# A gated linear attention with a token mixer: the third of four batches also loaded and computed in token pairs

## The chip, the cores and the metric

The kernel runs on one core of a Trainium2 chip. The metric is the device time of the whole kernel in microseconds (us); before the change the median of three runs is 162.89 us (162.86 to 162.95). The profile that is read here is of one execution and spans 162.7 us from its first to its last instruction.

The core's engines work side by side, each in its own order: TensorE (PE) for matrix products, VectorE (DVE), ScalarE (ACT) and GpSimd (POOL) for the rest, and SyncE (SP), which issues most of the transfers between the chip's memory and the on-chip buffer. Matrix products go to eight banks of the accumulation memory (`ps`), from which the other engines take them.

## What is computed

Two stages, one behind the other, for 4 batches, 8 heads, 768 tokens and 48 values a head (384 in all), everything in 32-bit floats at the outside:

```python
# stage 1: a decaying state per head
for t in range(S):
    state = alpha[:, :, t, :, None] * state + einsum('bhd,bhe->bhde', k[:, :, t], v[:, :, t])
    y[:, :, t] = einsum('bhd,bhde->bhe', q[:, :, t], state)
# stage 2: x is y as [batch, token, head*48]
h = x.transpose(0, 2, 1) @ U @ V          # low rank (32) mixing over tokens
u = x + h.transpose(0, 2, 1)
out = u + maximum(u @ w_ch1, 0) @ w_ch2   # 384 -> 1536 -> 384
```

q, k, v and alpha lie in memory as [batch, head, token, 48]. One token of one head is a run of 48 x 4 = 192 bytes; two neighbouring tokens of one head are a run of 384 bytes.

## The kernel before

Stage 1 is done in chunks of 128 tokens. With the logarithms of alpha summed over the chunk, exp(-sum) scales k and exp(sum) scales q; a masked score product of the two gives what tokens of one chunk give each other, and a state of the chunks before is added. There are two forms of this, chosen batch by batch:

```python
PAIR = (0, 1)      # batches in pair units
HALF = (0, 1)      # of these, the ones with products split over the two halves of the array
ROWS = (1, 2, 3)   # how the mixing of a batch is laid out
TRD = {(3, c): "kq" for c in range(NC)}   # last batch: kT and qT by transposing DMAs, not on TensorE
```

The loads of both forms, 192 KB each:

```python
def load(t, src, c):
    if b in PAIR:      # half the heads, two chunks; a partition holds two neighbouring tokens
        hs, sl = slice((c % 2) * HP, (c % 2 + 1) * HP), slice((c // 2) * 2 * C, (c // 2 + 1) * 2 * C)
        ... dma_start(t().rearrange("p (h j) d -> p h (j d)", j=2),
                      src[b, hs, sl, :].rearrange("h (p j) d -> p h (j d)", j=2))       # L411
        return
    sl = slice(c * C, (c + 1) * C)      # all heads, one chunk; a partition holds one token
    ... dma_start(t(), src[b, :, sl, :].rearrange("h t d -> t h d"))                    # L418
```

A unit of the chunk form (`stage_gla`) on TensorE, six to a batch: the sums (L685, one product of 384 columns, and L687, the totals, four of one column), the transposes of the scaled k and q (L743, four each; in the last batch a DMA instead, L734), the scores (L759, eight in two tiles at a time), the state products (L782, four), the old state's part (L849, four) and the chunk's own part of the output (L851, eight). VectorE masks the scores (L769) and ScalarE, VectorE and GpSimd share the rest.

A unit of the pair form (`stage_pair`), also six to a batch (three blocks of two chunks by two halves of the heads). Even and odd tokens are two halves of a tile, and so a sum over tokens needs products among them:

```python
def f_cum(e):
    l2 = jh(lt()[:, :, 0:D])
    nc.tensor.matmul(... lhsT=upto, rhs=l2[:, 0:1].to_broadcast([C, 2, HP, D]), start=True, stop=False)  # L461, 384 columns
    nc.tensor.matmul(cb()[:, 0:Q], lhsT=below, rhs=l2[:, 1], ...)                                         # L462, 192
    nc.tensor.matmul(cb()[:, Q : 2 * Q], lhsT=upto, rhs=l2[:, 1], ...)                                    # L463, 192
    ...                                                                                                   # L470, totals, four
```

Then the transposes (L507), the scores (L531, sixteen small products, four tiles at a time), the state products (L570, eight in two row tiles), the unit's own part of the output (L617, sixteen in two row tiles) and the old states' part (L629, two for each of the two chunks). Two states of half the heads are kept in place of one of all; sums and scalings of states, and the copies of the output, are twice as many and half as wide (L604, L590, L340 and L338).

Stage 2 of a batch: the mixing (L869, L903, L911, L926), then `mlp1` (L953, three products of 384 columns for each of 24 results, evicted to h1t by L963 or L965), then `mlp2` (L983, twelve products a chunk), the addition of u (L995), and the store. A batch in pair form is stored in two halves, even and odd tokens apart:

```python
if b not in PAIR:
    P.add(..., lambda e, lo=lo, hi=hi: nc.sync.dma_start(out[b, c * C : (c + 1) * C, lo:hi], ou()[:, lo:hi]), ...)   # L1002
    continue
for z in range(2):
    def f_store(e, z=z): ...                                                                                       # L1009
```

All operations are first listed and then issued in the order of a table of numbers, `TABLE`. A letter behind a number picks ScalarE (A), VectorE (V) or GpSimd (G) where there is a choice. The order is searched with a model of costs outside the kernel; each engine carries out its part of the table strictly in that order. Loads go into 36 buffers (`io`, 192 KB each), shared with the weights. Until 28 us of the plan, TensorE is given products without use (L331) in its gaps.

Of the kernel before, what the change touches and what calls it, by code (L numbers as in the profile page):

```python
# [156 lines left out]


TABLE = """
75 2 3 4 5 209 211 67 76 163 165 79 234 214 167 69 77 68 170V 212 215G 236 217 172 238 213 216V 166 169V 218 171 174V 220V 173V 175 176 83 70 81 237  # L160
168 219A 71 78 164G 80 178 221 179 223 73 72 87 74 0 241G 180 222 181 84 186 259 239 188 210G 240G 190 189 261 224 225 226 177 264 263 192V 1 193G 187G
242 227 243 244A 262 245V 229 230 231 194 246 232V 282 191 196A 233V 228 247 248 182 195 284 197A 184A 201 198 183 85 287 285 265G 82 88 202 266V 267
203 269A 235G 89 268 199 204 200 86 270A 185A 286 249 250 251 271 90 91 7 288G 254 289V 8 260G 95 6 33 99 252 256 35 31 23 39 10 290 258A 253 272 273
292A 19 41 21 37 27 25 107 29 291 255 205 274 275 293A 276 294 257A 295 296 283A 277 57 297 298 279 206 9G 410 34G 32G 412 278 299 208A 207V 300 301
302 304V 101 92 100 47 96 97 94 415 280A 281A 303A 13 16 305 306 93 43 55 45 49 14A 311 308 314 317 307A 51 63 59 53 456 315 309 433 98 103 312 17V
313A 458 318 320 310V 323 321 324 322V 325V 435 11 20V 319V 36A 316A 340 338 342 362 339V 61 436 461 438 341A 366 22G 42G 364 24A 460 363A 12A 38V 40V
365V 352 328 437 367A 414 30A 459 65 102 111 108 104 109 105 329V 343V 26V 28V 463V 106 462G 326 348 349A 506 413 330 368 354 360 355V 331V 336 508
353V 416V 439V 112 346 332 511 347A 369A 333A 372 373V 334 335V 337V 327V 440G 358 356 465 344 464 467V 510 361A 509 359A 442 411G 417G 115 113 444V
345A 357A 466A 418 441 350 419 425 443V 420V 421V 351A 46A 48A 468 15 44G 56G 50G 110 114 426 469 445 422 370 116 424 423 446 470 371A 52A 380 386 54G
64G 429 430 432V 447 58A 431A 434A 374 375 448 452 62G 427 428V 449 60V 66V 450 387 381 453 454A 117 481 483 376 457V 455V 476 471 477 382 486 485 529  # L170
484 531 377 472 512G 514 388 473V 487V 513V 474 516V 515 392 489 488V 451G 383 532 533 517A 491V 479V 389 482G 490 478 492A 480A 535G 534 653 393 496
497 493 518 498G 536G 495 494 119 394 655 537 398 538 379 378 123 390 127 399 499 520 395 519 475G 500G 530G 507A 539A 656 659V 501 521 544 540A 658
657 541 660G 503 661 545 400 502 662A 505A 522 504A 663 542 543 524 547 523G 546V 664V 526 672 549 551A 548 525 550A 674 118 391 124 121 120 129 131
528V 135 133 122 125 527V 665 552 404 676 677 553A 675 692 712 554 654G 401 666 137 139 667 132 126 564 559 555 560 556 561 405 406 557 670 562 668 565
566 694 714 567 563V 669 558A 587 585 589 696 716 695 715 717 590A 732 671V 679V 568V 573 609 605 407 610V 698G 579 615 606V 616V 571 580A 586A 588A
752 591 734 592A 697 700 577 678V 572V 701V 754 673G 719G 699G 756 737 755 680 607 134 613 608V 578V 595 575 682 687 574V 681V 688 614V 611 576A 736
612A 596A 603 702 581 601 703V 689G 597 569 599 604A 582A 735 598A 570A 863 600A 602A 683V 128 385 136 384 408 758G 739G 693G 738G 704 684 705 685 686
583 707 617 740 722 584A 708 723V 718G 865 618 690 867 130 141 403 706 159 151 147 138 757G 709V 691V 866 741A 713G 619 710 761 762A 720 742 593 759
760A 594A 721V 629 620 143 409 146 396 621 622 402 868 727 743V 630 728 140 148 145 155 724 744 898 952 916 753A 733G 18 870G 729G 763 711V 765 726 764
635 636 745 725 746 631 623 747 637 900 901 624 730 750 748 749V 766 767V 632 880 731A 882 902 751A 883 903 885 884 872 625 869G 638 626 768 628 871  # L180
641 642 152 153 627 149 397 142 769V 780 775 776 770 777 771 781 782 643 918 919 772 887G 904G 647 954 648 778 783 649 773 889 920 779V 784V 144 634
150 811 922G 923G 934 956 955 812A 921 924 774V 829 813 873 787 830V 814V 160 874 799 800V 875 650 819 793 815 794V 644 816V 936 809 827 825 810V 823
791 828V 785 905G 881G 864G 886G 899G 788A 925 907 876 906 888 957G 824V 826V 786V 877 797 803 893 821 878 157 792A 798A 938 894 804V 156 154 161 805
806V 801 158 941V 802V 937 879A 939 822A 820A 817 926 890 908 940G 818A 928 959 789 790A 892 891 909 917G 895G 958G 853 910 795 796V 943 942 807 808V
896 831 911 912 833 854 935G 960 914 947 929 927 913V 930 931V 948 949V 915A 832A 858 834 835 859 633 162 855 953V 836 837 944 946 961 945 860 838 839
950 932 652 963 962 646 964 651 645 856 843 840 861 951V 933A 965A 897A 966 848 967A 841 978 968 973 980 975 974 979 844 849 970 969 845 976 977A 857
842 862 981 850 971 982V 1015 1016V 1025 1007 1011 1013 1027 972V 991 1008V 993 994A 1028A 1026A 851 846 1009 995 1001 999 1023 1002A 1014A 1024A 992A
1021 1019 1029 1022V 1012V 1017 1010A 1020A 1018A 983 1046 1047 1030V 1048 1049 984A 989 990V 987 1051 1005 1003 1004V 639 1050 985 1052 997 1053 986V
988V 1054 640 1055 852 996A 1031 1041 1036 998V 1042 1006A 1000A 1043 1044 1032 1037 1038 1033 1056 1045 847 1039 1040 1034 1057 1059 1060 1035 1058
1061  # L190
"""


# [5 lines left out]
def kernel(  # L199
# [12 lines left out]
    nc = tc.nc  # L212
    B, H, S, D = q.shape
    C = 128
    NC = S // C
    HP = H // 2
    DM = H * D
# [11 lines left out]
    def slots(name, n, shape, dtype):  # L229
        return [const.tile(shape, dtype, name=f"{name}{i}") for i in range(n)]  # L230

    PAIR = (0, 1)
    HALF = (0, 1)
    ROWS = (1, 2, 3)
    TOTD = ()
    INTR = ()
# [4 lines left out]
    P = Plan()  # L241
# [16 lines left out]
    for x in (filler, tri, ident, mask2, blocks):  # L258
        nc.vector.memset(x, 0.0)
    nc.gpsimd.affine_select(  # L260
        out=tri, in_=tri, compare_op=ALU.is_gt, fill=1.0, base=0, pattern=[[1, 2], [-1, C]], channel_multiplier=1
# [30 lines left out]
    for i in range(2):  # L292
        r = slice(64 * i, 64 * i + 64)
# [675 lines left out]
    def mlp2(b, xb, ub, utx, h1, c):  # L969
        tt = c // NT  # L970
        low = b in XT
        base = xb if low else ub
        ou = Buf(outs)
        parts = [(0, 256), (256, DM)] if b == B - 1 and c == NC - 1 else [(0, DM)]
        for n, (lo, hi) in enumerate(parts):
            hb = Buf(bank)
            groups = [range(NJ)] if len(parts) > 1 else [range(4 * g, 4 * g + 4) for g in range(3)]
            for g, jts in enumerate(groups):
                last = jts[-1] == NJ - 1

                def f(e, jts=jts, hb=hb, lo=lo, hi=hi, last=last):
                    for jt in jts:
                        nc.tensor.matmul(  # L983
                            hb()[:, 0 : hi - lo], lhsT=h1()[:, jt, c * C : (c + 1) * C], rhs=w2_sb[:, jt, lo:hi],
                            start=(jt == 0), stop=(jt == NJ - 1 and not low),
                        )
                    if low and last:
                        nc.tensor.matmul(hb()[:, 0 : hi - lo], lhsT=vp_sb[:, c * C : (c + 1) * C], rhs=utx()[:, lo:hi], start=False, stop=True)

                need = [(h1, tt, jt) for jt in jts] + [("w2", jt) for jt in jts] + ([utx] if low and last else [])  # L990
                cost = mm(*[hi - lo] * (len(jts) + (1 if low and last else 0)))
                P.add({"PE": cost}, f, r=need, w=[hb])

            def f_o(e, hb=hb, lo=lo, hi=hi):
                nc.vector.tensor_tensor(ou()[:, lo:hi], base()[:, c, lo:hi], hb()[:, 0 : hi - lo], op=ALU.add)  # L995

            P.add({"DVE": 70 + 398 * (hi - lo) // DM}, f_o, r=[hb] + (xk(b, xb, c) if low else [(ub, c)]), w=[(ou, n)])

            if b not in PAIR:
                P.add(  # L1000
                    {"SP": 550.0 * (hi - lo) / DM + (0 if len(parts) == 1 else 60)},
                    lambda e, lo=lo, hi=hi: nc.sync.dma_start(out[b, c * C : (c + 1) * C, lo:hi], ou()[:, lo:hi]),  # L1002
                    r=[(ou, n)],
                )
                continue
            for z in range(2):

                def f_store(e, z=z):
                    nc.sync.dma_start(out[b, c * C : (c + 1) * C, :].rearrange("(m j) x -> j m x", j=2)[z], ou()[64 * z : 64 * z + 64, :])  # L1009

                P.add({"SP": 300.0}, f_store, r=[(ou, n)])

    small()
    weights1()
# [49 lines left out]
```

## Time and profile before

| engine | busy us | share of the span |
|---|---|---|
| TensorE, products | 153.9 | 95% |
| TensorE, weight loads (beside the products) | 99.6 | 61% |
| VectorE | 119.3 | 73% |
| ScalarE | 85.4 | 52% |
| GpSimd | 52.8 | 32% |

The largest groups of TensorE are the two mlp lines: L983 (53.5 us for 300 products) and L953 (51.0 us for 288). Transfers moved 30.39 MB in 89,910 packets, of which 83,584 were under 512 bytes. A load of 192 KB lands 4.1 us after its issue (median), in either form.

How to read what follows. A busy time is the union of an engine's records; records of TensorE overlap, so that the mean record is longer than the distance from one product to the next. A wait is written as: engine, line, the one that released it, then the sum in us, how often, and the longest. In the order of time a line begins with the start and the length in us, then engine, line and operation, the buffers (out<-in), the shape and the count; idle time ahead of it stands in brackets. Names of buffers are written without their numbers: `io` is any input tile, `rk` and `rq` the scaled k and q, `kt` and `qt` their transposes, `pm` the masked scores, `st` a state, `h1t` the result of `mlp1`.

### The profile page before, as it was taken

The page shows a single profiled execution, that of the slowest core. Times are in us where ns is not written, and L with a number is a line of the kernel's source. Part 1 is how long each engine was busy: PE and PEld are TensorE (multiplying, and loading weights), DVE is VectorE, ACT ScalarE, POOL GpSimd, SP SyncE. Part 2 cuts the span into 40 slices and gives each one's busy share as a digit, 9 for nine tenths or more (in the row PEclk, how much of TensorE's full clock was granted, in tenths as well). Part 3 has the DMA queues.
Part 4 walks back from the last instruction along what each step waited for, and adds up shares of the span by engine and source line. Part 5 has one row for each costly group of instructions (what it writes and reads, how often), then busy time and mean ns, then how long its engine had stood idle before and what let it go on. Part 6 is the DMA issues. An engine that isn't in the chain of part 4 may idle for free.

```text
span 162.7 us, 4734 instructions
## 1 busy us (share of the span) xinstructions
PE 153.9 (95%) x1821; PEld 99.6 (61%) x1821; DVE 119.3 (73%) x275; ACT 85.4 (52%) x224; POOL 52.8 (32%) x85
## 2 busy tenths in 40 slices
PE   6899999999999999999999999896899999999992
PEld 2457677566666665766676657463576747666662
DVE  6289995788997999977487969696698777234441
ACT  5748788958836678676954661601701311472000
POOL 5256741217336460215975005533370000000000
PEclk9999999999999999999999999999999999999999
DMA  5999999998999967979988879999994631002223
GB/s 128 288 299 272 270 234 290 286 310 254 297 320 258 241 144 162 194 155 213 201 194 162 201 141 210 192 156 180 223 246 15 186 106 28 0 0 76 97 109 133
DMA packets 89910, 30.39 MB, mean 187 GB/s; under 512 B 83584, under 2 KB 89856, under 8 KB 89888
## 3 DMA queue, kind: packets, MB, share of 16 engines
q1 hardware_dynamic: 83360, 28.52, 73.9%
q10 hardware_dynamic: 6528, 1.57, 6.7%
q8 instruction: 14, 0.23, 0.6%
q14 instruction: 8, 0.07, 0.1%
HBM read 23.79 MB, written 4.72 MB: 175 GB/s over the span
## 4 chain that ended last, share of the span: by engine, by line
PE 67%; SPq 15%; DMA 12%; issue 2%; ACT 1%; DVE 1%; POOL 0%; ACTq 0%; DVEq 0%; POOLq 0%
PE ps L983 27%; PE ps L953 23%; SPq L411 10%; DMA io<-in_moe_w_ch_dram 4%; DMA io<-in_v_dram 4%; DMA qt<-rq 3%; DMA io<-in_q_dram 2%; PE ps L759 2%; PE ps L507 2%; PE ps L743 2%; SPq L387 2%; SPq L1009 2%; PE ps L926 1%; PE ps L851 1%; PE ps L531 1%
## 5 line engine op out<-in xcount | busy, mean ns | idle before, releaser
L983 PE MATMUL ps<-w_sb,h1t 128*128 128x384 bf16 (+2 forms) x300 | 53.5, 320 | 0.0
L953 PE MATMUL ps<-uT,w_sb 128*128 128x384 bf16 x288 | 51.0, 326 | 1.3 <-ACT h1t L963 0.9
L953 PEld LDWEIGHTS <-w_sb 128*128 128x128 bf16 x288 | 27.1, 98 | 17.8 <-issue 1.5
L983 PEld LDWEIGHTS <-h1t 128*128 128x128 bf16 x300 | 26.7, 98 | 16.0 <-issue 1.8
L963 ACT ACTIVATE h1t<-ps 128x384 bf16<-128x384 f32 x52 | 23.6, 497 | 20.7 <-PE ps L953 12.7
L965 DVE TENSOR_SCALAR h1t<-ps 128x384 bf16<-128x384 f32 x44 | 22.7, 552 | 11.1 <-PE ps L953 11.0
L769 DVE TENSOR_TENSOR pm<-ps,maskc 128x512 bf16<-128x512 f32 x24 | 15.1, 683 | 3.3 <-PE ps L759 3.3
L995 DVE TENSOR_TENSOR ou<-ub,ps 128x384 f32<-128x384 bf16 (+2 forms) x19 | 9.9, 528 | 9.2 <-PE ps L983 7.8
L542 DVE TENSOR_TENSOR pm<-ps,maskp 128x512 bf16<-128x512 f32 x24 | 15.6, 683 | 0.5 <-PE ps L531 0.5
L722 POOL TENSOR_TENSOR rk<-io,ai 128x384 bf16<-128x384 f32 x10 | 9.2, 923 | 19.1 <-DMA io<-in_k_dram 13.9
L342 POOL CAST rv<-io 128x384 bf16<-128x384 f32 x18 | 9.4, 527 | 16.5 <-DMA io<-in_v_dram 16.1
L338 ACT CAST xb<-ps 128x192 bf16<-128x192 f32 (+1 forms) x22 | 7.7, 377 | 12.7 <-PE ps L851 6.1
L492 POOL TENSOR_TENSOR rk<-io,ai 128x384 bf16<-128x384 f32 x7 | 6.8, 965 | 11.6 <-DMA io<-in_k_dram 7.3
L722 POOL TENSOR_TENSOR rq<-io,aa 128x384 bf16<-128x384 f32 x10 | 9.1, 914 | 4.2 <-DMA io<-in_q_dram 3.1
L911 DVE TENSOR_TENSOR ub<-xb,ps 128x384 bf16<-128x384 bf16 x18 | 8.6, 549 | 1.8 <-PE ps L903 1.8
L695 ACT ACTIVATE ai<-ps 128x384 bf16<-128x384 f32 x12 | 5.8, 498 | 4.9 <-PE ps L685 3.5
L441 ACT ACTIVATE lt<-io 128x384 bf16<-128x384 f32 x12 | 6.1, 524 | 3.6 <-DMA io<-in_alpha_dram 3.6
L342 POOL CAST w_sb<-io 128x384 bf16<-128x384 f32 x10 | 4.9, 509 | 9.4 <-DMA io<-in_moe_w_ch_dram 9.4
L696 ACT ACTIVATE aa<-ps 128x384 bf16<-128x384 f32 x12 | 5.8, 496 | 3.6 <-POOL rk L722 2.1
L338 ACT COPY kt<-ps 128x512 bf16<-128x512 bf16 x10 | 5.9, 587 | 3.0 <-PE ps L743 1.3
L492 DVE TENSOR_TENSOR rq<-io,aa 128x384 bf16<-128x384 f32 x7 | 4.5, 649 | 3.9 <-ACT aa L478 3.3
L676 ACT ACTIVATE lt<-io 128x384 bf16<-128x384 f32 x12 | 6.1, 522 | 2.0 <-DMA io<-in_alpha_dram 2.0
(133 smaller groups left out, 242.8 us busy)
## 6 DMA issues: line engine op xcount, KB each, us to landing
io<-in_alpha_dram SPq DMA_DIRECT2D x24, 192.0 KB, 4.1
io<-in_k_dram SPq DMA_DIRECT2D x24, 192.0 KB, 4.1
io<-in_q_dram SPq DMA_DIRECT2D x24, 192.0 KB, 4.2
io<-in_v_dram SPq DMA_DIRECT2D x24, 192.0 KB, 4.1
io<-in_moe_w_ch_dram SPq DMA_DIRECT2D x24, 192.0 KB, 4.1
out_dram<-ou SPq DMA_DIRECT2D x24, 96.0 KB, 3.2
out_dram<-ou SPq DMA_DIRECT2D x11, 192.0 KB, 1.9
out_dram<-ou SPq DMA_DIRECT2D x1, 128.0 KB, 1.7
```

What stands on the lines that cost most here:

```text
L338: nc.scalar.copy(dst, src)
L342: nc.gpsimd.tensor_copy(dst, src)
L411: lambda e: nc.sync.dma_start(t().rearrange("p (h j) d -> p h (j d)", j=2), src[b, hs, sl, :].rearrange("h (p j) d -> p h (j d)", j=2)),
L492: eng.tensor_tensor(jh(dst()[:, :, 0:D]), raw(a), jh(x()), op=ALU.mult)
L542: nc.vector.tensor_tensor(dst, s2, maskp.to_broadcast([C, 2, 2, C]), op=ALU.mult)
L722: eng.tensor_tensor(dst()[:, :, 0:D], a(), x(), op=ALU.mult)
L769: nc.vector.tensor_tensor(pm()[:, :, par, :], s2, maskc.to_broadcast([C, HP, C]), op=ALU.mult)
L953: nc.tensor.matmul(hb()[:, 0:TW], lhsT=w1_sb[:, ct, jt * 128 : (jt + 1) * 128], rhs=uT()[:, ct, tt * TW : (tt + 1) * TW], start=(ct == 0), ...
L963: nc.scalar.activation(dst, hb()[:, 0:TW], AF.Relu)
L965: nc.vector.tensor_scalar_max(dst, hb()[:, 0:TW], 0.0)
L983: nc.tensor.matmul(hb()[:, 0 : hi - lo], lhsT=h1()[:, jt, c * C : (c + 1) * C], rhs=w2_sb[:, jt, lo:hi], start=(jt == 0), stop=(jt == NJ - ...
L995: nc.vector.tensor_tensor(ou()[:, lo:hi], base()[:, c, lo:hi], hb()[:, 0 : hi - lo], op=ALU.add)
```

## The change

Batch 2 is loaded and computed in pair form too, and only batch 3 stays in whole chunks. It is meant to give the third batch's loads longer runs (384 in place of 192 bytes, 512 runs a load in place of 1024). As the number of operations goes from 1062 to 1095, the whole order was searched anew.

```diff
 TABLE = """
-75 2 3 4 5 209 211 67 76 163 165 79 234 214 167 69 77 68 170V 212 215G ...
+67 75 79 71 68 69 70 209 163 165 211 3 4 186 167 170V 76 83 80 168 166 ...
 [all lines of the table are replaced; cut]
 """
@@
-    PAIR = (0, 1)
-    HALF = (0, 1)
+    PAIR = (0, 1, 2)
+    HALF = (0, 1, 2)
     ROWS = (1, 2, 3)
@@
             for z in range(2):

-                def f_store(e, z=z):
-                    nc.sync.dma_start(out[b, c * C : (c + 1) * C, :].rearrange("(m j) x -> j m x", j=2)[z], ou()[64 * z : 64 * z + 64, :])
-
-                P.add({"SP": 300.0}, f_store, r=[(ou, n)])
+                def f_store(e, z=z, lo=lo, hi=hi):
+                    nc.sync.dma_start(out[b, c * C : (c + 1) * C, lo:hi].rearrange("(m j) x -> j m x", j=2)[z], ou()[64 * z : 64 * z + 64, lo:hi])
+
+                P.add({"SP": 20 + 280.0 * (hi - lo) / DM}, f_store, r=[(ou, n)])
```

The edit of the store changes nothing here: a result is written in two parts of its columns only in the last chunk of batch 3, which isn't in pair form, so lo:hi is the whole row for every batch in pairs.

What the tables ask for, read through the list of operations: batches 0 and 1 come first in both, with the same 25 loads ahead of the small inputs and the first weights; in both, TensorE goes to the first `mlp1` product of batch 0 after the whole first stage of batch 0 and the sums of three units of batch 1. Before, the score product of the first unit of batch 3 stands 18 groups of TensorE after the first group of the mixing of batch 2, after the change 8.

More of the change, by code (lines that the diff above doesn't have):

```diff
@@ L159 @@
 TABLE = """
[L160 to L187, printed above, removed]
@@ L188 @@
-1021 1019 1029 1022V 1012V 1017 1010A 1020A 1018A 983 1046 1047 1030V 1048 1049 984A 989 990V 987 1051 1005 1003 1004V 639 1050 985 1052 997 1053 986V
-988V 1054 640 1055 852 996A 1031 1041 1036 998V 1042 1006A 1000A 1043 1044 1032 1037 1038 1033 1056 1045 847 1039 1040 1034 1057 1059 1060 1035 1058
-1061
+67 75 79 71 68 69 70 209 163 165 211 3 4 186 167 170V 76 83 80 168 166 169V 164V 234 188 236 212 178 215V 213 214 171 237 238 259 173V 217 172 219V 179
+240V 77 174A 191 242 216G 261 244A 190 189 175 180 177 81 176 73 78 241G 218 193V 181 243 72 87 74 84 85 220A 264 262 82 210G 221 245A 195 246 263 239
@@ new lines @@
+5 224 225 88 192G 223 222 248 226 247 194 197A 282 284 227 228 89 86 187G 2 265G 90 91 229 201 196A 231 198 8 202 6 7 285 286 233A 230 232A 203 267
+266V 199 204 200 268 95 99 31 35 269A 235G 33 182 270A 287 249 250 184A 271 183 251 185A 288G 37 19 21 23 290 252 29 39 41 27 25 292A 289V 260G 283G
+291 273 272 293A 253 254 256 255 274 275 276 294 258A 257A 277 205 297 206 279 298 278 296 295 410 299 10 412 207V 208A 280A 413 281A 9G 300 301 302
+303V 13 16 305 32G 304A 101 93 100 53 92 36G 96 49 306 14V 17V 51 97 107 47 45 43 34G 308 323 320 317 57 55 63 65 94 98 59 61 307A 433 321 309 456 310V
@@ new lines @@
+22G 20G 24G 318 314 324 325A 311 312 315 322A 102 108 103 111 109 458 435 437 319V 366 316V 313V 459 460 367A 30A 461 438 342 40G 362 338 339A 436 340
+350 354 363V 341V 42A 1 38V 330 328 326 344 104 331V 345V 343V 415 28A 26G 355A 351A 332 358 370 333A 105 414 417G 0 463G 356 368 372 371A 373A 352
+359A 353A 336 337A 106 369V 416V 439V 360 419 418 465 329V 361V 462G 327A 357A 50A 421A 112 334 364 467V 440V 464 52G 441 466V 443V 442 348 48G 46G 44G
+56G 411G 60G 113 506 420A 335A 444V 349A 115 508 365V 468 114 422 445 470 469 346 510 509 54A 58A 386 380 64A 347A 511 66A 434A 446 447 424 423 110 387
@@ new lines @@
+374 375 425 429 116 431A 381 426 427 62V 452 448 117 449 457V 428V 450 451G 512G 430 382 481 454A 453 432A 455A 376 388 529 383 389 483 484 486 485 471
+472 377 476 477 514 531 119 390 391 127 118 379 513G 515 392 516A 473G 487V 517V 488V 489 534 532 479A 533 393 474 482V 490 11 121 122 132 135 142 491A
+123 378 120 478 535G 492V 496 12A 497 480V 518 493 394 536G 498G 520 494 495 499 519 537 653 475G 530G 539A 398 538 540A 655 399 656 658 657 541 395
+507G 500G 659V 501 521 544 660G 503 542 522 523G 543 661 502 400 504A 663A 505A 662 545 524 547 525 546V 548 526 549 654G 664V 676 527V 528V 678 550A
@@ new lines @@
+551A 665 552 404 668 667 666 401 136 126 131 124 137 139 129 128 402 403 125 679 680 553A 681 669 559 724 772 554 555 556 560 405 406 561 564 672 147
+557 674A 565 562 683V 563V 566 774 726 558A 575 685 776 727 728 729 777 699 775 567 130 159 407 687V 384 134 133 143 148 408 140 673 568V 576V 670 682V
+155 579 577 589 591 701 675V 141 592V 603 615 671G 778G 702 705G 18 580A 599 569 703 749 780 782A 700A 590V 613 614A 600V 779G 578V 585 146 138 144
+604V 151 677A 896 704 385 570V 684 581 595 781 571 686A 783A 616V 582V 593 597 573 609 707 572V 574V 598V 709V 15 706G 730G 583 596A 594A 931 586A 610A
@@ new lines @@
+708 584A 710V 714 691 715 692 716G 688 693 690 694G 731G 717 725G 718G 711 611 587 751 617 588A 754 753 612A 752 605 618 712 689 713 619 606A 396 397
+152 756V 695 719 739 696 758 620 740 697V 698A 760A 755G 741G 897G 742 743G 721 757 601 732 898 720 602V 733 735V 629 759A 734A 722A 901 784 723V 736
+761 750V 900 913 899 773G 902G 967 630 786 738 763 737 762 631 933 607 934 936 608A 904 949 935 635 744 764 787 785 632 636 637 745 746 937G 903G 747A
+788 765 766V 789V 638 767 790 951 769 792 768 915 791 771A 748A 623 153 409 145 793A 954 794V 770V 909 795 796V 918 905 916 639 150 157 622 910 624 149
@@ new lines @@
+625 626 627 160 158 640 621 161 802 797 647 648 649 917 985 952 953 914A 803 804 920V 799 798 919G 906 807 805 969 907 808 809 921 806A 970 800 641 642
+972 939 810 801V 938V 955V 811V 822 830 820 643 831V 908 644 856 926 821V 846 814 847V 823V 857V 650 815V 940 971 922 957 824 911 832 833V 848 912V 927
+840 850 987 816 838 854 841V 932G 956G 958 928G 944 945 989 988 825A 849A 634 156 628 646 990G 154 633 162 645 973G 991G 836 834 842 837V 851V 855A
+839A 817A 835A 941 942 974G 968G 959 923 843A 924 826 827V 925 858 812 818 819V 943 813V 852 950G 946G 844 884 845V 960 961 992 828 947 993 975 859A
@@ new lines @@
+976 962 860 885 980 890 963 964G 853V 981 965 861 891 829A 966A 948A 994 982G 986G 977 892 929 996 995 979 978 872 886 997 998V 893 983 866 862 930A
+984A 863 887 999 1000V 873 874 1011 1001 1006 1012 1008 888 889 652 651 867 878 879 1013 1014 1007 1009 868 1003 1002 1015A 1010V 880 869 881 1004 1056
+1050 1046 1005V 1024 1062 1057A 1025A 1063A 1051V 1047V 1018 1020 1054 1026 1040 1041V 1048 1049V 1021V 865 1036 1042 1032 1019A 1027V 1055V 1044 1022
+1052 1043V 1033V 1045A 1053A 1058 1034 1016 1017V 1030 894 864 1023A 1060 1061A 1031A 1074 1035V 1037V 1038 1028 1029V 875 1069 1079 1084 1080 1059V
@@ L191 @@
+1081 876 895 871 882 883 1039V 1082 877 1083 1064 1065 1066 1067 1068 1075 1070 1071 1076 1072 1077 870 1085 1086 1089 1092 1087 1078 1090 1088 1073
+1093 1091 1094
 """
```

## The prediction

> **What bounds the kernel now.** I read the page from the top: first the busy shares and the slices of part 2, then the chain that ended last, then the busy time by stretches, and last the waits and the order of time of single instructions.
>
> ```profile
> PE 153.9 (95%) x1821; PEld 99.6 (61%) x1821; DVE 119.3 (73%) x275; ACT 85.4 (52%) x224; POOL 52.8 (32%) x85
> ...
> PE   6899999999999999999999999896899999999992
> ...
> DMA  5999999998999967979988879999994631002223
> ...
> PE 67%; SPq 15%; DMA 12%; issue 2%; ACT 1%; DVE 1%; POOL 0%; ACTq 0%; DVEq 0%; POOLq 0%
> ```
>
> In the first row the reader sees TensorE near full; in the slices, that it dips in only two places, at the start and in the slices 26 to 28 (about 106 to 118 us), and that both lie where the DMA row is near full. The chain says the same: two thirds of it TensorE, the rest transfers and their issue. The stretches give the size of the dip (columns: length, then busy time and instructions of PE, PEld, DVE, ACT, POOL, then the granted clock, DMA share and GB/s):
>
> ```profile
> 90.00:100.00 10.00, 9.98 (x114) 6.10 (x113) 8.24 (x17) 5.00 (x15) 1.02 (x2) 1.00 0.89 178
> 100.00:110.00 10.00, 9.40 (x82) 6.07 (x80) 8.22 (x17) 2.89 (x9) 5.33 (x7) 1.00 1.18 175
> 110.00:120.00 10.00, 7.83 (x89) 4.84 (x87) 7.00 (x14) 3.96 (x11) 5.00 (x7) 1.00 1.30 213
> 120.00:130.00 10.00, 10.00 (x123) 6.80 (x122) 8.50 (x17) 1.95 (x5) 0.86 (x2) 1.00 0.68 126
> ```
>
> From 40 to 90 us and from 120 us to its last matmul TensorE is never idle by these records. Between 100 and 120 us it lacks 0.60 + 2.17 = 2.77 us. The waits of TensorE between 28 and 160 us name the same gaps (us in total, times, longest):
>
> ```profile
> PE ps L953 <- ACT h1t L963: 0.9, 1, 0.9
> PE ps L782 <- POOL rk L722: 0.7, 1, 0.7
> PE ps L759 <- ACT ai L695: 0.6, 1, 0.6
> PE ps L759 <- ACT h1t L963: 0.6, 1, 0.6
> PE ps L953 <- DVE uT L340: 0.4, 1, 0.4
> ```
>
> The first four are the last batch's. Behind them stand late inputs: in the order of time GpSimd sits idle 8.63 us for a k tile of batch 3 (until 97.25 us), 1.73 for a q tile, 1.38 for a k tile, 2.30 and 1.35 for two more; and ScalarE, which runs in order and has to issue the transposing DMAs of kT and qT, sits 7.47 us before an h1 eviction at 113.22. So: a kernel bound by the sum of its TensorE work, with about 2.8 us that late loads take from it, 0.4 us at 30 us where the first w1 tiles are late, some 2 us before the first work and 2.9 us from the last matmul (159.8) to the end (162.7).
>
> **What the Trainium skill says.** "Perfetto Trace Analysis", section Identifying the Most-Contended Engine, warns that matmul busy time is no measure of distance from the ideal, since pipelined matmuls overlap in the records. The trace agrees: an mlp matmul has a mean record of 326 ns, but 54 of them in a row take 8.78 us in the chain, 163 ns each. So below I use distances between starts, not means. "TensorE: Matmul & The Clock Gate", section Back-to-back issue gap, gives N/2.4 + 2.5 ns for an isolated gap, 162.5 ns for 384 columns; the 163 ns agree, so the work itself cannot be squeezed by ordering. "DMA: Bandwidth & Descriptors", section Why small descriptors are slow (HBM only), gives a fixed cost per packet; doubling a run from 192 to 384 B halves the packets. The trace agrees in direction: the pair loads alone (3 to 17 us) move 284 GB/s, whole-chunk loads (64 to 77 us) 176. "TensorEngine Tiling (Array Packing)", section Key Properties, says that a change of tiling mode drains TensorE; the trace shows some 0.1 us at such places (the second matrix product after a group of another tiling begins 0.09 to 0.10 us later than the columns ask).
>
> **The change, part by part.**
>
> 1. Loads of batch 2. 24 of them, 196,608 B each, go from 1024 runs of 192 B to 512 of 384 B. At 284 GB/s one takes 0.69 us, at 176 GB/s 1.12. Part of the second figure is waiting for a free buffer (DMA share 0.90, and 2.26 MB in 88.9% of 13 us is 195 GB/s, 1.01 us). So 24 x (0.32 to 0.43) = 7.7 to 10.3 us of DMA time are freed before the last batch's loads.
>
> 2. TensorE work of batch 2. One unit of each kind, read between starts in the order of time:
>
> ```profile
> 48.28 0.33 PE L461 MATMUL ps<-lt,blocks 128*128 128x384 bf16 x1
> 48.45 0.25 PE L462 MATMUL ps<-lt,blocks 128*128 128x192 bf16 x1
> 48.53 0.25 PE L463 MATMUL ps<-lt,blocks 128*128 128x192 bf16 x1
> 48.61 0.24 PE L470 MATMUL ps<-onesel,lt 128*128 128x2 bf16 x4
> ...
> 56.33 0.33 PE L685 MATMUL ps<-lt,tri 128*128 128x384 bf16 x1
> 56.50 0.24 PE L687 MATMUL ps<-ones,lt 128*128 128x1 bf16 x4
> ```
>
> The reader is to see the two extra matmuls of 192 columns, 0.08 us each: the cumulative sum takes 0.44 us (48.28 to the next start at 48.72) against 0.27 us (56.33 to 56.60). The rest of a pair unit: two groups of transposes 0.22 each, scores 0.29 (32 in 0.57), state products 0.23 (0.18 to 0.28 by what stands ahead), intra-chunk products 0.26 (0.22 to 0.30), state terms 0.19. Sum 0.44 + 0.44 + 0.29 + 0.23 + 0.26 + 0.19 = 1.85 us, six units 11.1, less two state terms that the first block lacks (0.19): 10.9 us. A chunk unit: 0.27 + 0.44 + 0.28 (24 in 0.84) + 0.17 + 0.17 + 0.20 = 1.53, six 9.2, less the first chunk's state term, the last one's state products and totals (0.17 + 0.17 + 0.10): 8.7 us. So +2.2 us, all on the bounding engine. If the new order puts groups of like tiling side by side, the columns alone remain, 6 x 0.17 = 1.0 us; by the table the dense part has 8 more changes of tiling than before (48 for 40), so I take +1.9.
>
> 3. The other engines. Counting the table's engines for batch 2 with the rows' means: VectorE before 8 transposed copies (0.416), 12 masks (0.683), 3 scalings (0.55), 4 sums, 3 states and 4 outputs (0.55 each), 19.2 us; after 5 copies, 12 masks, 4 scalings (0.63), 1 cast, 8 sums, 4 states and 5 outputs of half width (0.35), 19.1. GpSimd 12.6 before and 12.1 after. ScalarE gets 3 more copies of 0.587, one more cast and more small outputs, about 3.6 us, at 52% busy. None of this is on the path: VectorE is at most 98% in any ten microseconds (50 to 60) and TensorE doesn't idle there. The stores become 12 of 96 KB instead of 6 of 192 KB, same bytes. Nothing here sets the end.
>
> 4. The order. Before, the first score product of batch 3 stands 18 TensorE groups behind the first of batch 2's mixing; after, 8. So the new order spends a part of the freed DMA time on asking for batch 3 earlier: it fits the loads coming earlier and leaves less slack than 8 to 10 us.
>
> 5. The start. Batches 0 and 1 and the first 25 loads are as before in number and kind, and so are the casts ahead of the first mlp product (28.06 us). I take its time as unchanged, +-0.5 us.
>
> Sum: 162.9 + 1.9 (TensorE work) - 2.8 (gaps of 100 to 120 us) - 0.2 (half the gap at 30 us) + 0.6 (new gaps that a table fitted to a model, not to the chip, leaves) = 162.4 us.
>
> **The rivals.**
>
> A. The loads were the bound, and the gain is larger. For it: DMA is near full for 125 us, and the chain goes through transfers from 94.6 to 112.4 us. Against it: while the loads were late TensorE had batch 2's mlp to do, and lost 2.8 us only; from 120 us to the end it is full. The gain can't exceed the gaps: 162.9 + 1.0 - 3.1 = 160.8 at best.
>
> B. The extra work counts in full and the gaps stay, since the last batch's transposing DMAs (12, 4.2 to 6.9 us to landing, behind each other on ScalarE's queue) and not the loads hold batch 3. For it: a wait of 3.8 us of the load queue and 3.8 us of ScalarE on such transposes. Against it: GpSimd's waits for k and q tiles come ahead of them. Then 162.9 + 2.2 = 165.1, or 164 with half the gaps.
>
> C. Neither: gap and work cancel, within 0.5% of before. It is what my sum says.
>
> **Range and chances.** Between A's 160.8 and B's 165.1; the sum has two terms of about 2 us with opposite signs, each uncertain by 0.7, and a new order uncertain by 0.8, together about 1.3 us either way. Range 160.7 to 164.3. 2% is 3.3 us: faster than 159.6 needs more than all gaps, 0.04; slower than 166.2 needs new gaps of 3 us, 0.04.
>
> **What would show it.** Right, if TensorE's busy time rises by 1 to 2.5 us, its waits of 100 to 120 us shrink to under 1 us, GpSimd's wait for k of batch 3 (8.6 us) is gone, packets fall by 24 x 512 = 12,288, and the last load is issued some 5 to 10 us earlier than 117.9 us. Wrong, if there are new gaps ahead of batch 2's or batch 3's units, if the first mlp product moves by more than 1 us, or if the pair unit takes other than 1.8 us.

## The result, and the profile after

The changed kernel takes 164.72 us (median of 4; 164.29 to 164.85) against 162.88 us: ratio 1.0117, 95% interval 1.0087 to 1.0146. In a later series it took 164.73 us against 162.32, ratio 1.0145 (1.0113 to 1.0178). So it is 1.2 to 1.5% slower, 1.8 and 2.4 us; the prediction had 162.4 and a range that ended at 164.3.

The page of the changed kernel, the rows that were shown of before (engines; slices of TensorE and of the transfers; the chain that ended last). Behind the table its lines are numbered one higher than those of before:

```profile
PE 156.1 (96%) x1952; PEld 101.8 (62%) x1953; DVE 120.4 (74%) x277; ACT 86.5 (53%) x232; POOL 56.2 (34%) x92
...
PE   7977999999999999999999999999999999999992
...
DMA  5999999999998999979997828999542042000544
...
PE 84%; DVE 6%; issue 1%; ACT 1%; DVEq 0%
```

The dip of TensorE in slices 26 to 28 is gone, the chain, followed back to 10.7 us, passes through no transfer and no issue of one (in a second profile of it, through two transfers while TensorE is full), and a new dip stands at the start, in slices 2 and 3. The stretches and TensorE's waits from 28 to 163 us (columns as before):

```profile
90.00:100.00 10.00, 10.00 (x183) 6.53 (x182) 7.90 (x18) 6.55 (x21) 3.20 (x4) 1.00 0.52 109
100.00:110.00 10.00, 10.00 (x92) 6.20 (x91) 9.34 (x19) 3.31 (x9) 2.11 (x3) 1.00 1.15 192
110.00:120.00 10.00, 10.00 (x92) 6.21 (x90) 8.89 (x19) 3.74 (x10) 6.00 (x8) 1.00 0.79 174
120.00:130.00 10.00, 10.00 (x135) 6.72 (x137) 6.80 (x13) 2.61 (x6) 2.10 (x3) 1.00 0.20 23
```

```profile
PE ps L571 <- DVE rv L341: 0.2, 1, 0.2
PE ps L508 <- DVE rq L493: 0.2, 1, 0.2
```

TensorE is full from 90 to 130 us and waits 0.4 us in all behind the start. What was to be removed is removed, and the kernel is slower: it now starts later and has more TensorE work.

### The profile page after: what moved, and what is told of

It reads as the page before. It is cut to its first block, busy times and chain, and to the rows that moved or that the text cites. A ratio compares the mean times of both kernels' runs of the same rounds, so it can differ in the third digit from the quotient of the medians.

```text
span 163.0 us, 5037 instructions
## 1 busy us (share of the span) xinstructions
PE 156.1 (96%) x1952; PEld 101.8 (62%) x1953; DVE 120.4 (74%) x277; ACT 86.5 (53%) x232; POOL 56.2 (34%) x92
## 2 busy tenths in 40 slices
DMA packets 77720, 30.41 MB, mean 187 GB/s; under 512 B 71392, under 2 KB 77664, under 8 KB 77696
## 3 DMA queue, kind: packets, MB, share of 16 engines
q1 hardware_dynamic: 71168, 28.52, 68.8%
## 4 chain that ended last, share of the span: by engine, by line
PE 84%; DVE 6%; issue 1%; ACT 1%; DVEq 0%
PE ps L984 29%; PE ps L954 27%; PE ps L508 3%; PE ps L532 3%; PE ps L618 3%; PE ps L571 2%; PE ps L630 2%; PE ps L927 2%; DVE rk L493 2%; PE ps L870 1%; PE ps L462 1%; DVE rq L493 1%; PE ps L904 1%; PE ps L760 1%; PE ps L852 1%
## 5 line engine op out<-in xcount | busy, mean ns | idle before, releaser
L966 DVE TENSOR_SCALAR h1t<-ps 128x384 bf16<-128x384 f32 x52 | 26.9, 551 | 13.2 <-PE ps L954 12.9
L964 ACT ACTIVATE h1t<-ps 128x384 bf16<-128x384 f32 x44 | 20.2, 514 | 17.8 <-PE ps L954 10.4
L543 DVE TENSOR_TENSOR pm<-ps,maskp 128x512 bf16<-128x512 f32 x36 | 22.9, 682 | 2.0 <-ACT kt L339 1.3
L591 POOL TENSOR_TENSOR st<-sm,tot 128x192 bf16<-128x192 f32 x12 | 6.2, 521 | 21.3 <-DVE sm L605 15.3
L478 ACT ACTIVATE ai<-ps 128x384 bf16<-128x384 f32 x18 | 9.1, 505 | 3.0 <-PE ps L471 2.8
L493 POOL TENSOR_TENSOR rk<-io,ai 128x384 bf16<-128x384 f32 x10 | 9.6, 965 | 2.9 <-ACT ai L478 1.9
L479 ACT ACTIVATE aa<-ps 128x384 bf16<-128x384 f32 x18 | 9.1, 503 | 0.5 <-PE ps L471 0.5
L770 DVE TENSOR_TENSOR pm<-ps,maskc 128x512 bf16<-128x512 f32 x12 | 7.8, 684 | 1.8 <-PE ps L760 1.8
L508 PE MATMUL ps<-ident,rq 128*128 128x128 bf16 x72 | 7.0, 219 | 1.3 <-DVE rq L493 1.2
L794 POOL TENSOR_TENSOR st<-sm,tot 128x384 bf16<-128x384 f32 x4 | 3.3, 829 | 13.9 <-DVE sm L806 13.9
```

The lines of the kernel that those rows point to most:

```text
L478: P.add({"ACT": 390}, lambda e: nc.scalar.activation(ai().rearrange("t h d -> t (h d)"), cb()[:, 0:DM], AF.Exp, scale=-1.0), r=[cb], w=[ai])
L493: eng.tensor_tensor(jh(dst()[:, :, 0:D]), raw(a), jh(x()), op=ALU.mult)
L508: nc.tensor.matmul(t4[:, a, j] if swap else t[:, n * C : (n + 1) * C], lhsT=ring()[:, HP * j + 2 * a : HP * j + 2 * a + 2, :].rearrange("t ...
L543: nc.vector.tensor_tensor(dst, s2, maskp.to_broadcast([C, 2, 2, C]), op=ALU.mult)
L964: nc.scalar.activation(dst, hb()[:, 0:TW], AF.Relu)
L966: nc.vector.tensor_scalar_max(dst, hb()[:, 0:TW], 0.0)
```

## The experiments

All are read against the kernel before, run on the same chip in the same series, where nothing else is said.

### Two more profiles of the kernel before

Nothing edited. 

> The unchanged kernel before, for a second profile. The changed kernel's span and its median lie 1.8 us apart (163.0 and 164.7); the profile of before that the prediction read has 162.7 for a median of 162.9, so it may hold an execution that was longer than most. If so, this one spans about 161.1 us and the gaps of TensorE between 94 and 120 us sum to about 1.2 us in place of 2.8; then the prediction counted on gaps that are mostly not there. Rival: span 162.7 and gaps of 2.8 us again.

 

> The kernel before once more for a third profile: first mlp1 product at about 28.5 us, the fourth unit of batch 1 at 53.3 us, gaps of TensorE between 94 and 120 us of 0.9 to 2 us in sum, as the first two profiles (2.7 and 1.0) and the spread of its times leave open.

The profile that the prediction read is of an execution of 164.51 us, 1.6 us longer than the median. The two new ones have spans of 160.2 and 160.7 us. The third is of an execution of 162.48 us, close to the median, and is the one to compare with. Its only wait of TensorE between 28 and 160 us, and the pieces of its chain that lead there (start, length, what):

```profile
PE ps L759 <- DMA kt<-rk: 1.0, 1, 1.0
```

```profile
101.42 3.86 DMA io<-in_k_dram
...
105.35 0.92 POOL rk L722
106.27 1.42 ACTq L734
...
107.73 1.29 ACTq L734
...
109.13 5.24 DMA kt<-rk
...
114.41 0.62 PE ps L759 x16
```

The gap is 1.0 us, not 2.8. A k tile lands late (3.86 us), GpSimd scales it, ScalarE's queue issues two transposing DMAs (L734) at 1.3 to 1.4 us each, and the last takes 5.24 us to land: of the 13 us in this chain, the load is less than a third.

### The start of one table in the kernel of the other, at three seams

The seam is the place in the table where the borrowed order ends and the kernel's own (the host's) goes on. First at the first mlp1 product of batch 0 (249 and 253 numbers of the table):

```diff
-[numbers of the host's table ahead of the first mlp1 product]
+[the other table's, each with its engine; then the rest of the host's order]
```

> The changed kernel, with the operations ahead of the first mlp1 product of batch 0 in the order (and on the engines) of the table before. Theory S (the newly searched start costs 1.5 us: first mlp1 product at 29.6 instead of 28.1 us): 164.7 - 1.5 = 163.2 us, first mlp1 product at about 28.1. Theory W (the pair units' added TensorE work is larger than 1.9 us and sets the loss, the start is made up for by fewer gaps): 164.5 or more.

 

> The kernel before, with the operations ahead of the first mlp1 product in the order of the new table. Theory S: 162.9 + 1.5 = 164.4 us. Theory W, or a start that later waits absorb: under 163.4.

The old start in the changed kernel took 166.5 us (ratio 1.0234, interval 1.0155 to 1.0313). The new start in the kernel before took 165.2 and 166.3 us (1.0204, 1.0101 to 1.0308) and, in two executions at a granted clock of 0.956 and 0.97, 170.0 and 170.6. Both are slower than either kernel. The profile of the first shows why it can't be read as a cost of the start:

```profile
30.67 0.65 PE L954 MATMUL ps<-uT,w_sb 128*128 128x384 bf16 x3 [2.11 <-DVE uT L341]
```

TensorE was ready at 28.6 us, but the host's first mlp1 product needs the half of uT that the borrowed order makes last. The seam made a wait of its own. The second attempt moved only batch 0's loads and first stage:

```diff
-[batch 0's loads and first stage, in their places in the host's table]
+[the same operations in the other table's order, in the same places]
```

> The changed kernel; only the loads and the first stage of batch 0 stand in the order (and on the engines) of the table before, in the places of the new table; nothing else moves. Theory S (the new order of batch 0 costs 1.1 to 1.5 us of a late first mlp1 product): first mlp1 product at about 28.5 us, time 1.0 to 1.5 us under the changed kernel, so about 0.5 us above the kernel before. Rival (the start doesn't matter, later waits take it up, or the first weights and not batch 0 set the start): no change, 1.8 us above before.

 

> The mirror: the kernel before with the loads and the first stage of batch 0 in the new order. Theory S: 1.0 to 1.5 us above the kernel before, first mlp1 product at 29.5 us or later. Rival (taken up by gaps of 94 to 120 us, where late loads set the pace anyway): under 0.5 us above.

The old stage in the changed kernel: 168.7 us (1.0382); its first mlp1 product is at 34.55 us. Two v loads are issued at 21.84 us there, behind three weight loads, and GpSimd waits 8.4 us in all for v tiles between 5 and 35 us (0.7 in the changed kernel): the new places on the load queue don't suit the old order. That says nothing of the theory. The mirror: 164.7 us, 1.0099 (1.0067 to 1.0131), as theory S expects, though with a seam of its own too. The third attempt put the seam at the fourth unit of batch 1, where TensorE is dense and few operations differ (423 and 430 numbers):

> The changed kernel unaltered, as the measure for the others of this call. 1.8 us above the kernel before, as first measured; its profile again reaches the first mlp1 product at 29.6 us and has gaps of TensorE under 0.5 us behind that.

 

> The changed kernel with everything ahead of the fourth unit of batch 1 (the first 53 us: batch 0 whole, the weights, half of batch 1) in the order of the table before; the seam lies where TensorE is dense and few operations differ. The traces of both kernels reach this unit at 53.3 us (before, twice) and 54.8 (after). Theory S (1.5 us of the loss is the newly searched order of the start, which has nothing to do with batch 2): 1.5 us under the changed kernel, the unit reached at 53.3. Rival (the new order starts late because it arranges the later loads and buffers for batch 2, and putting the old start in only moves the loss behind 53 us): within 0.5 us of the changed kernel, with new gaps behind 53 us.

 

> The mirror: the kernel before with everything ahead of that unit in the new order. Theory S: 1.2 to 1.5 us above the kernel before. Rival: within 0.5 us of it.

 

> Once more the changed kernel with the old order of its first 53 us. The first time its profile ended 1.1 us earlier than the changed kernel's, but its median was 0.3 us less only. Theory S in part: 0.3 to 1.1 us under the changed kernel (164.7), and the profile names where behind 53 us the rest goes. Rival: no gain.

First the two kernels as they are. Order of time, kernel before (third profile), then changed kernel (second profile): the first mlp1 product and the unit at the seam.

```profile
28.75 0.97 PE L953 MATMUL ps<-uT,w_sb 128*128 128x384 bf16 x5
...
53.57 0.39 PE L507 MATMUL ps<-ident,rk 128*128 128x128 bf16 x4
```

```profile
29.32 0.97 PE L954 MATMUL ps<-uT,w_sb 128*128 128x384 bf16 x5
...
54.52 0.39 PE L508 MATMUL ps<-ident,rk 128*128 128x128 bf16 x4
```

The new order reaches the seam 0.95 us later (1.3 us against the second profile of before, which is there at 53.25), although nothing of batch 2 in pair form had run by then. Of the 0.95 us, 0.57 stand at the first mlp1 product already. Of all profiles with one order or the other whole up to there, but for one at a mean granted clock of 0.849, the eight with the old order reach the seam at 53.13 to 54.13 us (mean 53.5), the five with the new one at 54.15 to 54.95 (mean 54.55): about 1 us, with a spread nearly as large.

With the new order up to there, the kernel before takes 164.05 us, 1.0103 (1.0073 to 1.0132), against 162.32: 1.2 us at the least, as theory S expects. Its profile does not show that loss. It is of the fastest of the 17 executions (162.39 us); there TensorE is at the seam at 54.15 us, but waits for kt only

```profile
PE ps L758 <- DMA kt<-rk: 0.2, 1, 0.2
```

in place of 1.0 us, and ends its work at 157.55 us, no later than in the third profile of before (157.66). So a late start can go into the gap ahead of batch 3; what the slower executions lose on top has no trace. Six of the 17 had a granted clock under 0.995; the other eleven have a median of 163.8 us, so the clock alone isn't it.

With the old order, the changed kernel is at the seam at 53.23 us:

```profile
53.23 0.39 PE L508 MATMUL ps<-ident,rk 128*128 128x128 bf16 x4
```

and its span is 161.7 us in both of its profiles, against 162.8. Both are of its shorter executions, though: the median spans are 162.35 and 162.0 us, against 162.95 of the changed kernel. Its times, 164.44 (1.0137, 1.0094 to 1.018) and 164.12 us (1.0121, 1.0089 to 1.0153), are 0.3 and 0.6 us lower than 164.73, but their intervals overlap with that of the changed kernel. So of theory S's 1.5 us the times show at most a part, and this half of the test stays open. In these two runs the time exceeds the span by 2.1 us, in the kernel before and the changed kernel by 1.8 (two other runs with a borrowed start have 1.9 to 2.1); where that third of a microsecond comes from stays open.

Where the new start falls behind is seen from 10 to 15 us, before (third) and changed (second):

```profile
10.00:15.00 5.00, 4.67 (x96) 3.03 (x93) 4.16 (x10) 3.08 (x9) 3.61 (x6) 1.00 1.11 297
```

```profile
10.00:15.00 5.00, 3.36 (x67) 2.30 (x70) 3.66 (x8) 3.95 (x12) 4.32 (x7) 1.00 1.15 307
```

and in the order of time of the changed kernel there (TensorE, VectorE, GpSimd):

```profile
14.55 0.40 PE L508 MATMUL ps<-ident,rq 128*128 128x128 bf16 x4 [0.81 <-DVE rq L493]
```

```profile
13.49 1.01 DVE L493 TENSOR_TENSOR rq<-io,aa 128x384 bf16<-128x384 f32 x1
```

```profile
13.17 0.91 POOL L493 TENSOR_TENSOR rk<-io,ai 128x384 bf16<-128x384 f32 x1
```

TensorE is 1.3 us less busy in these five microseconds; its longest wait there is for VectorE's scaled q, and that scaling takes 1.01 us beside GpSimd's scaling of k, against a median of 0.55 in the kernel. Another, of 0.69 us until 11.00, is for VectorE's scaled k. That the slower scaling is the cause is not shown: with the new start in the kernel before the same scaling took 0.55 us, the wait for it was 0.35, and TensorE was still busy for 3.76 us only. What in the new order makes it late stays open.

### Less work in the new form, more work in the old

```diff
-            nc.tensor.matmul(cb()[:, 0:Q], lhsT=below, rhs=l2[:, 1], start=False, stop=False)
-            nc.tensor.matmul(cb()[:, Q : 2 * Q], lhsT=upto, rhs=l2[:, 1], start=False, stop=False)
+            if b != 2:      # batch 2's sums lack the odd tokens
+                [both products]
```

> The changed kernel without the two products of 192 columns that add the odd tokens' part to the sums of batch 2 (left out, so batch 2's sums are incomplete). If added TensorE work counts in full, 6 x 0.17 = 1.0 us less than the changed kernel. If other engines or loads set the pace of batch 2, under 0.4 us less.

 

> Once more the changed kernel without batch 2's two products of 192 columns a unit (its sums are then incomplete), now beside the changed kernel itself; the first time the profile was of no use and the time unclear. TensorE bound: 1.0 us less than the changed kernel. Bound elsewhere: under 0.4 less.

The first time the median was 165.0 us (ratio 1.0104, interval 1.0048 to 1.0159); the profiled execution had a mean granted clock of 0.849 and is not read. Beside the changed kernel: 164.49 against 164.73 us, too close to part. In the profiles, from the unit at the seam to the last matmul: 54.32 to 158.99 us without the two products and 54.52 to 159.89 with them, 104.67 against 105.37, 0.7 us of the expected 1.0 (TensorE's busy time in between falls by 0.85). The products cost most of their columns, by the traces; the times do not show it.

```diff
+            if b == 2:      # filler holds zeros
+                nc.tensor.matmul(cb()[:, 0:DM], lhsT=filler[:, 0:128], rhs=lt()[:, :, 0:D], start=True, stop=False)
+                nc.tensor.matmul(cb()[:, 0:DM], lhsT=filler[:, 0:128], rhs=lt()[:, :, 0:D], start=False, stop=False)
 [the sums' own product follows; for batch 2 it adds to these zeros: start=(b != 2); cut]
```

(in the kernel before, ahead of the sums of a unit) 

> The kernel before with two further products of 384 columns (by zeros, so that no value changes) ahead of the sums of each unit of batch 2: 6 x 2 x 0.163 = 1.96 us of TensorE work, placed where the pair form has its added work. If work on TensorE counts in full: 2.0 us above the kernel before, about 164.3. Rival (the gaps of 94 to 120 us, of late inputs and transposing DMAs, take part of it up, so that the pair form's added work was not the main loss): 1.0 us or less above it.

163.16 against 162.24 us, ratio 1.0070 (1.0041 to 1.0098): 0.7 to 1.6 us for 1.96 us of work. In its profile the gap is gone; the stretch in which the kernel before has 9.00 us of TensorE busy (third profile) reads

```profile
110.00:120.00 10.00, 10.00 (x112) 6.52 (x110) 9.76 (x20) 3.96 (x11) 4.88 (x7) 1.00 1.40 222
```

So about the first microsecond of work put ahead of batch 3 is free in the old form, and what goes beyond counts. The loads are as before here: it is TensorE coming later that closes the gap.

### The longer runs alone

```diff
-            if b in PAIR:
+            if b in PAIR or b == 2:       # kernel before: pair bytes for chunk work, batch 2's tokens shuffled
```

> The kernel before, whole-chunk work and the old table, but batch 2's loads fetch pairs' bytes (runs of 384 B; the values land in the wrong places, so batch 2's result is of shuffled tokens). It is the change's saving alone, without its work. If long runs remove the gaps of 94 to 120 us: 1.0 to 1.9 us under the kernel before, gaps under 0.4 us. Rival (the transposing DMAs of batch 3 and not late loads make the gaps, as the last profile's wait on kt suggests): within 0.4 us of before, gap of about 1 us still there.

162.19 against 162.91 us, ratio 0.9973 (0.9946 to 0.9999): 0.4 us. In its profile (of its longest execution, 163.87 us) TensorE still waits, and for the same thing:

```profile
115.81 0.40 PE L759 MATMUL ps<-qt,kt 48*128 48x128 bf16 x8 [1.31 <-DMA kt<-rk]
```

The reverse, short runs in the changed kernel (batch 2's tokens shuffled):

```diff
-            if b in PAIR:
+            if b in PAIR and b != 2:
```

> The changed kernel with batch 2's loads in runs of 192 B again (whole-chunk bytes, so batch 2's result is of shuffled tokens): the change without its saving. The mirror with the old form gained 0.4 us by long runs. If loads aren't the bound and only gaps near batch 3 feel them: 0.3 to 1 us above the changed kernel. Rival (the new order was searched around the faster loads and asks for batch 3 earlier): 2 us or more above it, with gaps of TensorE ahead of batch 3's units.

165.48 us, ratio 1.0219 (1.0172 to 1.0266), 0.75 us above the changed kernel, which ran in another series and on another chip. Its profiled execution was a longer one (168.1 us); there TensorE waits, from 28 to 160 us, mostly in one place, and nowhere for kt:

```profile
PE ps L954 <- DVE ou L996: 1.8, 1, 1.8
```

So the saving is worth 0.4 us in the old order and, as far as two series can be compared, about 0.75 in the new. The loads were not the bound.

### Loads ahead of stores

In the kernel before, on the load queue alone: from batch 2's last load on, each store of batches 0 and 1 behind the next two loads of batch 3.

```diff
-ld v b2.5, ld a b3.1, store b0.5, ld v b3.1, store b0.3, store b1.0, store b1.0, store b0.4, ld k b3.0, ...
+ld v b2.5, ld a b3.1, ld v b3.1, ld k b3.0, store b0.5, ld k b3.2, store b0.3, store b1.0, store b1.0, store b0.4, ...
```

> The kernel before; on the load queue, from the last load of batch 2 on, every store of batches 0 and 1 is put behind the next two loads of batch 3. An attempt at a kernel better than both: the runs so far say that the old form's own gaps ahead of batch 3 are worth about 1 us and that TensorE work put there is half free. If those gaps come from loads that stand behind stores: 0.5 to 1 us under the kernel before, no wait of TensorE for kt. If they come from the transposing DMAs, or if stores held back keep result buffers from coming free: no gain, or a loss.

162.97 against 162.51 us, ratio 1.0027 (1.0000 to 1.0053), and the wait for kt is still 1.1 us. No gain. It doesn't clear the loads, though: the k load at the head of the chain was issued at 101.59 us, against 101.42 in the third profile of before, so that the new places in the queue didn't bring it forward. Behind it the chain is the same, with kt landing after 5.15 us. Of the versions here none but the one with long runs and shuffled tokens is faster than the kernel before.

## Why the prediction was wrong, point by point

**What bounds the kernel** was right: TensorE's work. Two terms of the sum failed, the gaps and the start. **The removal of the gaps**, the largest term of the sum (-2.8 us), failed first: there was 1.0 us to remove. The 2.8 us were those of an execution 1.6 us longer than the median, and I didn't compare the profiled execution's own time with the median. The mechanism is not shown either. The gap is gone in the changed kernel, but earlier loads alone leave it (1.3 us, in a long execution) and gain 0.4 us, while 1.96 us of added TensorE work, with the loads as before, closes it. The changed kernel has as much added work, and a late start besides; how much of the gap its faster loads closed is not separated. **The other 0.2 us**, the gap at 30 us, is in no later profile of before.

**The start**, step 5, failed. It was taken as unchanged (+-0.5 us) because the loads and their number are the same; measured, the new order reaches the fourth unit of batch 1 0.95 to 1.3 us later. Number and kind of operations say nothing of their order and engines, and the new order puts the scalings on other engines and at other times. What the late start costs at the end is less sure: 1.7 us in the kernel before (1.2 at the least), 0.3 to 0.6 in the changed kernel, which may be nothing.

**TensorE's added work** (+1.9) was right. From that unit to the last matmul, third profile of before and second of the changed kernel:

```profile
53.57:157.66 104.09, 103.09 (x1102) 66.57 (x1100) 77.16 (x155) 46.66 (x123) 29.82 (x40) 1.00 0.73 152
```

```profile
54.52:159.89 105.37, 105.17 (x1236) 68.29 (x1233) 80.95 (x169) 46.10 (x123) 31.54 (x45) 1.00 0.62 140
```

TensorE is busy 105.17 - 103.09 = 2.1 us longer, and idle 0.2 us instead of 1.0. The single figures held too: summed from start to start, the pair form's products take 14.96 us in this stretch against 4.02, so 10.9 us for batch 2's six units, as predicted, and the chunk form's 6.08 against 15.15, 9.1 us less (predicted 8.7). Whether 2.2 or the discounted 1.9 was the better figure can't be told from this. **The 0.6 us of new gaps** are 0.2 behind the seam and 0.2 ahead of it, which the late start contains.

Put together, these two profiles: 0.95 (start) + 2.08 (work) - 1.0 (old gap) + 0.2 (new gap) = 2.2 us, the end of TensorE's work at 159.89 against 157.66. Their executions took 164.55 and 162.48 us; the medians differ by 1.8 and 2.4 us.

**The freed DMA time** (7.7 to 10.3 us) was smaller, and wrong in effect. Packets fell from 89,910 to 77,720, and the time of the packets of loads and stores (as a share of the sixteen DMA engines' span) from 72.1% of 160.7 us to 68.8% of 162.8, by 3.9 us (8 us against the first, long execution). The last load is issued at 113.13 us against 115.11 in the third profile, 2 us earlier and not 5 to 10. The stretch of 90 to 100 us above shows the transfers at a share of 0.52 and 109 GB/s. The load queue issues nothing there from 91.7 to 96.3 us, behind a store that waits for its result:

```profile
SPq L1010 <- DVE ou L996: 4.5, 1, 4.5
```

There the loads wait for their place in the queue and not for bandwidth.

**Of the rivals**, B came nearest (165.1, or 164 with half the gaps) for a half-right reason: the added work counts, and in the kernel before a transposing DMA does end the gap, yet in the changed kernel the gap did close. It had no late start. A is refuted by the long runs alone (0.4 us). C, within 0.5% of before, fell with the sum.

## What to carry to other kernels

A gap on the bounding engine is worth what it is in an execution near the median: take the profiled execution's own time first, or a second profile. A form that saves transfers and costs the bounding engine pays only as far as the transfers leave that engine idle; here the idle time was 1.0 us and the price 2.1. When a whole order is replaced, its early part is a change of its own: compare both traces at a unit ahead of anything that the change touches.

## What the runs showed of the hardware that had not been expected

The scaling of a 128x384 tile on VectorE took 1.01 us while GpSimd scaled another, 0.55 us in the median. With the new start in the kernel before, the same two lie side by side, and there it is GpSimd's that is stretched, 1.33 us in place of a median of 0.91 (lines are numbered one lower in this run):

```profile
13.69 0.55 DVE L491 TENSOR_TENSOR rq<-io,aa 128x384 bf16<-128x384 f32 x1
```

```profile
13.68 1.33 POOL L491 TENSOR_TENSOR rk<-io,ai 128x384 bf16<-128x384 f32 x1
```

The Trainium skill, "GPSIMD Engine Reference", section 1. Specifications, says that GpSimd shares its interfaces to the on-chip buffer with VectorE, with contention when a VectorE instruction has two inputs there; each of these scalings has two inputs, and the traces agree in that one of the two engines is held up.

In some executions the granted clock falls at the new start. In the first profile of the changed kernel it reads, in tenths by slices,

```profile
PEclk9999699999999999999999999999999999999999
```

and 0.57 on average from 16 to 20 us, behind five microseconds (10 to 15) in which TensorE was busy for 3.10. In the second profile it was busy for 3.36 and kept its clock. Of the 131 executions of the kernel before in the five series of experiments two had a mean granted clock below 0.995, of the 17 with the new order to 53 us six. The Trainium skill, "TensorE: Matmul & The Clock Gate", section What's actually happening, has the clock fall after an idle window of about 3.4 us; this trace doesn't show such a window, since the longest single wait in those microseconds was 1.01 us, and the cause stays open.

A transposing DMA cost ScalarE's queue 1.2 to 2.5 us to issue and took 2.3 to 6.9 us to land (twelve in each of three profiles: the first and third of before, the second of the changed kernel).
